# One set of seven PSUM banks, held as two three-bank tiles and one single tile, for every stage of an attention and gMLP block; output weights loaded in 14 pieces

## The chip, the core and the metric

The program runs on one core of a Trainium2 chip. The metric is the device time of one execution, in microseconds (us). The engines are TensorE (PE in the profile, with its weight loads as PEld), VectorE (DVE), ScalarE (ACT), GpSimd (POOL) and SyncE (SP, which here only issues transfers). Each engine works through its own list of instructions in order, and semaphores tie the lists together: an instruction that carries a wait holds up everything behind it on its engine.

## The reference

A sequence of 2048 tokens of width 448 goes through an attention block and then through a gMLP block, both with a layer norm whose shift and scale come from a small conditioning vector:

```
mod = silu(c) @ w_mod                        # sa, ca, ga, sb, cb, gb
h = layernorm(x) * (1 + ca) + sa
x = x + ga * attention(h)                    # 16 heads of 28, softmax over 2048 keys, then @ wo
h = layernorm(x) * (1 + cb) + sb
z = gelu(h @ w_in); z1, z2 = z[:, :896], layernorm(z[:, 896:])
g = w_sp @ z2 + b_sp                         # 2048 x 2048 mixing over the tokens
x = x + gb * ((z1 * g) @ w_out)
```

All of it is float32; most products are made of parts of float32r operands (a high part and a low part).

## The kernel before

The order of every engine's work is the order in which the Python code issues it; a recording layer adds the semaphores. It looks at which tile an instruction reads or writes, and makes a later user of that tile wait for an earlier one on another engine.

The stages, with the names that the profile shows:

- **Projection.** Values `pv`, queries and keys `pq` (`qk_unit`: groups of 11 matmuls into one PSUM bank, then read by ACT). From about 82 us on, the first score rows (`m_first`) stand between the matmuls of the remaining `qk_unit` groups.
- **Attention.** The loop runs over units `u`, 16 key tiles for each of 16 heads. A unit issues, in turn, four matmuls `st_ps` (`s_mm`; ACT reads each with an exponential into `P`) and four matmuls `mt` of a head 20 units later (`m_mm`; DVE reads each and keeps the row maximum in `pm`). Every second unit ends with the products of `P` and the values, `o_ps` (`pv_mm`). Two units, with 16 matmuls of `st_ps` and `mt` and one burst of `o_ps`, are called a pair below. The last 20 units have no `mt`.
- **Output projection, input projection, gate halves.** `wo_ps`, `z1_ps`, `z2_ps`: 11 matmuls into a bank, then a read by DVE or ACT.
- **Mixing.** The product with `w_sp` is built from 26 block products (`MIX`), each of four steps; step `g` runs from 0 to 103. `mix_step` issues nine matmuls into three banks of `accs`, and three more where the step also carries a piece of the last 128 columns (`F6_AT`). `w_load` brings raw blocks (`raw_sp`, five buffers), `w_split` makes high and low parts in `heapB`, and `evac` adds three banks at once to the result.
- **Output.** `y_part`: 21 matmuls for each of 16 token tiles into `y_ps`, then an add by DVE and a store.

All stages but the last two take their PSUM from `bank()`, which returns one of seven banks. In the first stages the list `banks` makes the seven go round; in attention the class `First` chooses the bank that a small table of due times says comes free first. Each call makes a new tile of one bank:

```
        return ring.tile([128, 512], F32, name=name, tag=f"b{k}")
```

So the tile that a matmul writes holds one bank, and what the matmul waits for is the reader of the tile that held this bank before, seven or so matmuls ago. Before the mixing the pool is closed, `accs` is made in a new one of eight banks (tiles of 3, 3, 1 and 1 banks), and after it that pool is closed too and `y_ps` gets a third one.

Of the kernel before, what the change touches and what calls it, by code (L numbers as in the profile page):

```python
# [8 lines left out]
F32 = mybir.dt.float32  # L9
F32R = mybir.dt.float32r  # L10
# [3 lines left out]
PSUM = bass.MemoryType.PSUM  # L14
DRAM = bass.MemoryType.DRAM

S, D, H, DH, FH = 2048, 448, 16, 28, 896
# [49 lines left out]
MIX = (  # L67
    (((T0, 4, 7, 1), (T1, 0, T0, 1)), T1, 1, 6, ((1, 1, -1), (1, 3, -1))),
    ((), T0, 1, 2, ((1, 0, 1),)),
    (((ONCE, 3, T1, 1),), ONCE, 1, 3, ((0, 2, 1),)),  # L70
    (((T1, 1, 2, 1), (ONCE, T1, T0, -1)), ONCE, 1, 11, ((0, 0, -1),)),
    (((ONCE, 0, T1, 1),), ONCE, -1, 19, ()),
    ((), T1, 1, 12, ((0, 1, 1), (1, 1, -1))),
    ((), 3, 1, 18, ((0, 0, -1), (0, 1, -1))),
    ((), 6, 1, (2, 1), ((1, 1, 1),)),
# [24 lines left out]
def tile_adaln_mha_gmlp(ctx, tc, x, wqkv, wo, w_in, w_spT, b_sp, w_out, cT, w_mod0, w_mod, out):  # L100
    nc = tc.nc
    ctx.enter_context(tc.manual_schedule())
    pe, dve, act, pool, sp = nc.tensor, nc.vector, nc.scalar, nc.gpsimd, nc.sync
# [11 lines left out]
    wo2_scr = scr.tile([2, 7, 128, D], F32, name="wo2_scr")  # L115
# [18 lines left out]
    def hview(heap, off, a, b):  # L134
        return heap[:, off : off + a * b].rearrange("p (a b) -> p a b", b=b)
# [68 lines left out]
    ps = ctx.enter_context(ExitStack())  # L204
    ring = ps.enter_context(tc.tile_pool(name="ring", bufs=1, space=PSUM))
    ps_o = ps.enter_context(tc.tile_pool(name="ps_o", bufs=1, space=PSUM))
# [17 lines left out]
    wms, xts, raws = {}, {}, {}  # L224


    banks, mode = list(range(7)), [None]

    def bank(name):
        k = mode[0](name) if mode[0] else banks[0]  # L230
        banks.remove(k)
        banks.append(k)
        return ring.tile([128, 512], F32, name=name, tag=f"b{k}")

    def load_mod(pair, eng):
        for k in range(4):
# [57 lines left out]
    accs = {}  # L294
# [552 lines left out]
    def w_block(k, j, kt):  # L847
        r = (4 * ROWS[k] + kt) * 128
        return w_spT[r : r + 128, j * 512 : (j + 1) * 512]
# [3 lines left out]
    def ws_tiles(i):  # L853
        if not ws_raw:
            ws_raw.append(dpool.tile([128, 7, 512], F32, name="ws_raw", tag="heapF"))
            ws_raw.append(spool.tile([128, 6, 512], F32, name="ws_raw2"))
        k = i % 6 if i < 100 else 3 + i % 3
        return [ws_raw[k // 3][:, 2 * (k % 3) + j, :] for j in range(2)]

    def ws_load(i):  # L860
# [113 lines left out]
    for u in range(NU + 1):  # L974
# [7 lines left out]
        if u % 2 and NU - LEAD < u < NU - 1:  # L982
            k = (u - NU + LEAD) // 2
# [26 lines left out]
    heapA = fh.tile([128, 8 * 896], F32R, name="heapA")  # L1010
# [161 lines left out]
    wouts = {}  # L1172
# [42 lines left out]

    wp = ctx.enter_context(tc.tile_pool(name="wp", bufs=4))
    FG = [slice(0, 384), slice(384, 768), slice(768, 896)]
    NM, KS = len(MIX), 4 * len(MIX)

    z6h = wp.tile([128, NT, 128], F32R, name="z6h", bufs=1)  # L1220
    heapA = fh.tile([128, 8 * 896], F32R, name="heapA2", tag="heapA")
    heapB2, tbuf = [], []
# [23 lines left out]
        return tbuf[1][:, f * D : (f + 1) * D]  # L1246

    def wouts_l(f):
        return tbuf[1][:, 3136 + f * D : 3136 + (f + 1) * D] if f < 4 else heapA[:, (f - 4) * 768 : (f - 4) * 768 + D]

    def wouts_load(i):
        if i == 0:
            tbuf.append(wp.tile([128, 5120], F32R, name="wouts", tag="tw", bufs=1))
            sp.dma_start(hview(tbuf[1], 0, 7, D).bitcast(F32), wo2_scr[0].rearrange("f p n -> p f n"))
            sp.dma_start(hview(tbuf[1], 3136, 4, D).bitcast(F32), wo2_scr[1, 0:4].rearrange("f p n -> p f n"))
        else:
            for f in range(4, 7):
                sp.dma_start(wouts_l(f).bitcast(F32), wo2_scr[1, f])

    zt = [dpool.tile([128, 8 * 896], F32, name=f"z2{i}", tag=f"heapD{i}") for i in range(2)]  # L1260
    z2 = [zt[i // 8][:, i % 8 * FH : (i % 8 + 1) * FH] for i in range(NT)]
# [1 line left out]
    once = []  # L1263
# [9 lines left out]
    def z_sum(p):  # L1273
        if p >= NM:
            return
        for d, a, b, op in MIX[p][0]:
            if d == ONCE:
                once[:] = [wp.tile([128, 4, 384], F32, name="once", bufs=1)]
            dve.tensor_tensor(out=z_reg(d), in0=z_reg(a), in1=z_reg(b), op=ALU.add if op > 0 else ALU.subtract)

    def z_parts(p):
# [20 lines left out]
        sub(dve, lo, src, hi)  # L1302

    F6_AT = {}
    for tb, gs, shared in (
        (1, range(4, 28, 2), 7),
        (2, (32, 34, 36, 38, 44, 45, 47, 48, 50, 51, 53, 54), 10),
        (0, [g for g in range(56, 80) if g % 3 != 1], None),
        (3, [g for g in range(80, 96) if g % 4 != 3], 24),
    ):  # L1310
        own = [k for k in (0, 3, 1, 2) if shared is None or k != MIX[shared][3][0]]
        for i, g in enumerate(gs):
            F6_AT[g] = (tb, own[i // 4], i % 4, False)
        if shared is not None:
            for kt in range(4):
                F6_AT[4 * shared + kt] = (tb, MIX[shared][3][0], kt, True)

    raws, wsp = {}, {}

    def w_load(g):  # L1320
        if g >= KS:
            return
        v, kt = MIX[g // 4][3], g % 4
        raws[g] = [wp.tile([128, 512], F32, name="raw_sp", bufs=5)]
        if isinstance(v, int):
            sp.dma_start(raws[g][0], ws_scr[4 * v + kt])
            if kt < 2:
                raws[g].append(w_part("p"))
                sp.dma_start(raws[g][1].bitcast(F32), wl_scr[2 * v + kt])
        else:  # L1330
            sp.dma_start(raws[g][0], w_block(*v, kt))
        if g in F6_AT and not F6_AT[g][3]:
            tb, k, kt, _ = F6_AT[g]
            raws["f", g] = [wp.tile([128, 512], F32, name="raw_sp", bufs=5)]
            sp.dma_start(raws["f", g][0], w_block(k, tb, kt))

    def w_split(g):
# [58 lines left out]
        if t in (13, 15):  # L1396
            w_split((t - 13) // 2)
    ph4.close()
    ps.close()
    pm = ctx.enter_context(ExitStack())  # L1400
    accs = pm.enter_context(tc.tile_pool(name="accs", bufs=1, space=PSUM))
    accs = [accs.tile([128, n, 512], F32, name=f"acc_{i}") for i, n in enumerate((3, 3, 1, 1))]

    cE = fh.tile([128, 4 * 896], F32, name="cE", tag="heapE")
    cC = fh.tile([128, 4 * 896], F32, name="cC", tag="heapC")
# [42 lines left out]
    z1s, nz = {}, [0, 0]  # L1448

    def z1_load():  # L1450
        if nz[0] < len(gates):
            f, tb = gates[nz[0]]
            z1s[f, tb] = wp.tile([128, 512], F32, name="z1l", tag="raw_sp", bufs=5)
            sp.dma_start(z1s[f, tb], z1_scr[f * 128 : (f + 1) * 128, tb * 512 : (tb + 1) * 512])
            nz[0] += 1

# [18 lines left out]
    ts_order = [8, 9, 10, 11, 4, 5, 6, 7, 12, 13, 14, 15, 0, 1, 2, 3]  # L1475
    x2t = {}

    def x2_load(t):
        x2t[t] = wp.tile([128, 512], F32, name="x2l", tag="raw_sp", bufs=5)[:, :D]
        sp.dma_start(x2t[t], x2_scr[t * 128 : (t + 1) * 128, :])  # L1480

    def y_part(t, end=False):
        ts, uT = slice(t % 4 * 128, t % 4 * 128 + 128), uTs[t // 4]
        y = ring.tile([128, 512], F32, name="y_ps", tag=f"y{ts_order.index(t) % 8}")
        for f in range(7):
            pe.matmul(y[:, :D], uT[:, f, ts], wouts_h(f), start=f == 0, stop=False)  # L1486
            pe.matmul(y[:, :D], uT[:, 7 + f, ts], wouts_h(f), start=False, stop=False)  # L1487
            pe.matmul(y[:, :D], uT[:, f, ts], wouts_l(f), start=False, stop=f == 6)  # L1488
        o = x2t.pop(t)
        for c, eng in ((slice(0, D), act),) if not end else ((slice(0, D // 2), act), (slice(D // 2, D), sp)):  # L1490
            dve.tensor_tensor(out=o[:, c], in0=o[:, c], in1=y[:, c], op=ALU.add)  # L1491
            eng.dma_start(out[t * 128 : (t + 1) * 128, c], o[:, c])

    GATE_AT = (71, 73, 75, 77, 79, 81, 82, 83, 94, 99, 100, 101, 102, 103)
    SPLIT_AT = {92: (6,), 96: (3, 4, 5), 98: (0, 1, 2)}

    for g in range(KS):
        p, kt = divmod(g, 4)
        w_load(g + 4)
        w_split(g + 2)  # L1500
        if kt == 0:
            if p:
                z_hi(p + 1)
                evac(p - 1)
        elif kt == 1 and p:
            z_lo(p + 1)
        elif kt == 2:
            z_sum(p + 2)
        if g == 5:
            z6_split(3)  # L1510
        if g < 4:
            b_load(utile(6, g), g)
        if g + 2 in GATE_AT:
            z1_load()
        if g in GATE_AT:
            gate()
        if g == 80:
            wouts_load(0)
        if g == 100:
            wouts_load(1)  # L1520
        if g in SPLIT_AT:
            u_split(2, SPLIT_AT[g])
        if g >= KS - 2:
            z1_load()
            x2_load(8 + g - (KS - 2))
        mix_step(g)

    evac(NM - 1)
    pm.close()
    ps2 = ctx.enter_context(ExitStack())  # L1530
    ring = ps2.enter_context(tc.tile_pool(name="ring2", bufs=1, space=PSUM))
    parts = {0: (1, (0, 1, 2)), 1: (1, (3, 4, 5)), 2: (1, (6,)), 4: (3, (3, 4, 5)), 5: (3, (0, 1, 2)), 6: (3, (6,))}
    parts.update({8: (0, (0, 1, 2)), 9: (0, (3, 4, 5)), 10: (0, (6,))})
    for k, t in enumerate(ts_order):
# [59 lines left out]
```

## Time and profile before

| | |
|---|---|
| median of three runs | 1409.01 us (1405.46 to 1410.49) |
| profiled execution, its own time | 1407.85 us |
| its span in the profile | 1405.9 us |
| PE busy | 1379.5 us, 98% |
| DVE busy | 1069.5 us, 76% |
| ACT busy | 805.4 us, 57% |
| POOL busy | 360.3 us, 26% |
| granted PE clock, mean of the span | 0.993 |

A busy PE means that some matmul was between its start and its modelled end; matmuls overlap in their pipeline, so the step from one start to the next is shorter than the duration of one. In the rows, `out<-in` names the tile written and the tiles read, and "waited for" names the work whose end released an engine.

### The profile page before, as it was taken

The page shows a single profiled execution, that of the slowest core. Times are in us where ns is not written, and L with a number is a line of the kernel's source. Part 1 is how long each engine was busy: PE and PEld are TensorE (multiplying, and loading weights), DVE is VectorE, ACT ScalarE, POOL GpSimd, SP SyncE. Part 2 cuts the span into 40 slices and gives each one's busy share as a digit, 9 for nine tenths or more (in the row PEclk, how much of TensorE's full clock was granted, in tenths as well). Part 3 has the DMA queues.
Part 4 walks back from the last instruction along what each step waited for, and adds up shares of the span by engine and source line. Part 5 has one row for each costly group of instructions (what it writes and reads, how often), then busy time and mean ns, then how long its engine had stood idle before and what let it go on. Part 6 is the DMA issues. An engine that isn't in the chain of part 4 may idle for free. (4 is left out here: it accounts for less than half of the span.)

```text
span 1405.9 us, 20520 instructions
## 1 busy us (share of the span) xinstructions
PE 1379.5 (98%) x7098; PEld 977.2 (70%) x7098; DVE 1069.5 (76%) x1688; ACT 805.4 (57%) x1472; POOL 360.3 (26%) x367
## 2 busy tenths in 40 slices
PE   9999999999999999999999999999999999978998
PEld 8888655555555555555555555888988888856798
DVE  7898888888888888888878842852478778976653
ACT  6633667777776667777766788553245545533311
POOL 2144344344444356546530021000110000000000
PEclk9999999999999999999999999999999999999999
DMA  8464766777676667777663012537307656767553
GB/s 293 140 176 167 212 183 204 208 216 230 201 238 199 205 206 243 219 228 228 202 188 84 22 31 74 184 127 234 112 16 246 203 178 204 235 207 238 173 155 125
DMA packets 136931, 254.28 MB, mean 181 GB/s; under 512 B 21688, under 2 KB 37178, under 8 KB 134282
## 3 DMA queue, kind: packets, MB, share of 16 engines
q1 hardware_dynamic: 134110, 248.79, 57.0%
q10 hardware_dynamic: 2718, 4.19, 0.8%
q8 instruction: 56, 0.92, 0.3%
q14 instruction: 47, 0.39, 0.1%
HBM read 174.53 MB, written 73.59 MB: 176 GB/s over the span
## 5 line engine op out<-in xcount | busy, mean ns | idle before, releaser
L713 DVE TENSOR_REDUCE pm<-mt 128x1 f32<-128x512 f32 x1024 | 631.4, 682 | 86.8 <-PE mt L708 86.7
L744 ACT ACTIVATE P<-st_ps 128x512 f32<-128x512 f32 x1024 | 515.7, 622 | 205.8 <-PE st_ps L740 204.9
L740 PE MATMUL st_ps<-qst,kst 128*128 128x512 f32 x1024 | 406.7, 407 | 0.0
L708 PE MATMUL mt<-kst,qst 128*128 128x512 f32 x1024 | 402.6, 393 | 0.0
L740 PEld LDWEIGHTS st_ps<-qst,kst 128*128 128x128 f32 x1024 | 191.8, 188 | 140.5 <-issue 93.1
L755 PE MATMUL o_ps<-P,V 128*32 128x512 f32 x2048 | 246.2, 598 | 0.0
L708 PEld LDWEIGHTS mt<-kst,qst 128*128 128x128 f32 x1024 | 193.0, 188 | 32.9
L868 POOL TENSOR_TENSOR ws_raw<-ws_raw 128x512 f32<-128x512 f32 x112 | 143.8, 1289 | 188.8 <-DMA ws_raw<-in_w_spT_dram 96.0
L1342 ACT ACTIVATE heapB<-raw_sp 128x512 fp32r<-128x512 f32 x156 | 96.6, 629 | 124.4 <-PE acc L1425 68.6
L755 PEld LDWEIGHTS o_ps<-P,V 128*32 128x32 f32 x2048 | 53.5, 109 | 121.9 <-issue 116.7
L1423 PE MATMUL acc<-heapB,heapA 128*128 128x512 f32 x312 | 123.7, 397 | 9.5 <-ACT heapB L1342 8.9
L1425 PE MATMUL acc<-heapB,heapA 128*128 128x512 f32 x312 | 123.4, 395 | 0.0
L150 DVE TENSOR_TENSOR heapB<-raw_sp,heapB 128x512 fp32r<-128x512 f32 x112 | 75.0, 688 | 47.1 <-ACT heapB L1342 46.4
L1424 PE MATMUL acc<-heapB,heapA 128*128 128x512 f32 x222 | 88.0, 396 | 6.7 <-DVE heapB L150 6.7
L1423 PEld LDWEIGHTS acc<-heapB,heapA 128*128 128x128 f32 x312 | 59.6, 191 | 24.4 <-ACT heapB L1342 10.9
L1425 PEld LDWEIGHTS acc<-heapB,heapA 128*128 128x128 f32 x312 | 59.7, 191 | 12.4
L403 PE MATMUL pq<-heapD,heapD 128*128 128x512 f32 x196 | 61.8, 390 | 0.0
L150 POOL TENSOR_TENSOR ws_raw<-ws_raw 128x512 fp32r<-128x512 f32 x44 | 56.6, 1287 | 3.5
L1424 PEld LDWEIGHTS acc<-heapB,heapA 128*128 128x128 f32 x222 | 42.3, 191 | 16.7 <-DVE heapB L150 7.9
L784 POOL TENSOR_TENSOR osb<-osb,rb 128x512 f32<-128x512 f32 x15 | 19.2, 1282 | 111.2 <-DMA rb<-r_scr 65.9
L170 POOL TENSOR_TENSOR rsz<-rsz,mhalf 128x1 f32<-128x1 f32 x16 | 14.2, 890 | 118.1 <-DVE rsz L169 118.1
L1361 ACT ACTIVATE z<-z_ps 128x448 f32<-128x448 f32 x32 | 17.4, 545 | 46.8 <-PE z_ps L1358 46.8
(220 smaller groups left out, 1653.8 us busy)
## 6 DMA issues: line engine op xcount, KB each, us to landing
ws_raw<-in_w_spT_dram SPq DMA_DIRECT2D x136, 256.0 KB
ws_scr<-ws_raw SPq DMA_DIRECT2D x112, 256.0 KB
ws_raw<-ws_scr SPq DMA_DIRECT2D x88, 256.0 KB
raw_sp<-ws_scr SPq DMA_DIRECT2D x88, 256.0 KB
raw_sp<-in_w_spT_dram SPq DMA_DIRECT2D x68, 256.0 KB
wl_scr<-ws_raw SPq DMA_DIRECT2D x44, 256.0 KB
kst<-qk_scr SPq DMA_DIRECT2D x45, 224.0 KB
qst<-qk_scr SPq DMA_DIRECT2D x45, 224.0 KB
```

Source lines behind the costliest of these rows:

```text
L150: eng.tensor_tensor(out=dst, in0=a, in1=hi.bitcast(F32), op=ALU.subtract)
L403: pe.matmul(pq, wqk[:, b, m * 128 : (m + 1) * 128], hT[g][:, a, :], start=j == 0, stop=j == NST - 1)
L708: pe.matmul(mt, qst[h % 3][:, t * 128 : (t + 1) * 128], kst[h % 3][:, kb * 512 : (kb + 1) * 512], start=True, stop=True)
L713: dve.tensor_reduce(out=pms[h][:, t, kb : kb + 1], in_=mt, axis=AX.X, op=ALU.max)
L740: pe.matmul(st, kst[h % 3][:, kt * 128 : (kt + 1) * 128], qst[h % 3][:, qb * 512 : (qb + 1) * 512], start=True, stop=True)
L744: act.activation(p, st, AF.Exp, scale=SCALE)
L755: pe.matmul(otile[h][32 * qb : 32 * qb + 32, :], V[:, kt, h, :], ptiles.pop((u, qb)), start=kt == 0, stop=kt == NT - 1)
L868: pool.tensor_tensor(out=a, in0=a, in1=b, op=ALU.add if W_SUMS[v][2] > 0 else ALU.subtract)
L1342: act.activation(hi, raw[0], AF.Copy)
L1423: pe.matmul(o, zh[:, c], hi, start=p < 2 and kt == 0, stop=False, skip_group_check=p > 1)
L1424: pe.matmul(o, zh[:, c], lo, start=False, stop=False, skip_group_check=p > 1)
L1425: pe.matmul(o, zl[:, c], hi, start=False, stop=kt == 3, skip_group_check=p > 1)
```

## The change

Five things are changed.

1. `bank()` no longer makes tiles. Three tiles are made once: `ring_a` and `ring_b` of three banks each, `ring_c` of one. `bank()` returns a view of one bank of these. Which bank is chosen is decided by the same lists and tables.
2. The pool stays open to the end. The mixing sums `accs` are the tiles `ring_a`, `ring_b`, `ring_c` and the bank that the values' products used; `y_part` takes views of the same banks.
3. The output weights are loaded by 14 transfers of one 128x448 piece each, at steps 46 to 99 of the mixing, in place of two large and three small ones at steps 80 and 100.
4. The buffers of the raw mixing blocks are seven, not five; the pieces of the last 128 columns are placed by a rule that keeps them apart; the gates (`GATE_AT`) stand at other steps.
5. The operand buffers of the weight sums (`ws_tiles`) go round by six to the end. Before, they went round by three from the hundredth on, and a block was loaded over one that had not yet been stored.

```
+    sums_a, sums_b = (ring.tile([128, 3, 512], F32, name=f"ring_{n}") for n in "ab")
+    ring_c = ring.tile([128, 512], F32, name="ring_c")
+    ring_v = [sums_a[:, k, :] for k in range(3)] + [sums_b[:, k, :] for k in range(3)] + [ring_c]
...
-        return ring.tile([128, 512], F32, name=name, tag=f"b{k}")
+        return ring_v[k]
...
-        k = i % 6 if i < 100 else 3 + i % 3
+        k = i % 6
...
+    WOUT_AT = [(46, 0, 0), (49, 0, 1), (52, 0, 2), (55, 0, 3), (58, 0, 4), (61, 0, 5), (64, 0, 6)]
...
+    def wouts_load(g):
+        for at_g, i, f in WOUT_AT:
+            if at_g == g:
...
+                sp.dma_start((wouts_l if i else wouts_h)(f).bitcast(F32), wo2_scr[i, f])
...
+        if f6_items and g not in F6_AT and (f6_items[0][0] in (1, 2) or g >= 47):
+            near = [range(max(a, 0), a + 3) for a in (g - 2, g - 1, g)]
+            if all(sum(own6(i) for i in w) < 2 and sum(lows(i) for i in w) < 4 for w in near):
+                F6_AT[g] = f6_items.pop(0)
...
-        raws[g] = [wp.tile([128, 512], F32, name="raw_sp", bufs=5)]
+        raws[g] = [wp.tile([128, 512], F32, name="raw_sp", bufs=RAWS)]
...
-    ps.close()
-    pm = ctx.enter_context(ExitStack())
-    accs = pm.enter_context(tc.tile_pool(name="accs", bufs=1, space=PSUM))
-    accs = [accs.tile([128, n, 512], F32, name=f"acc_{i}") for i, n in enumerate((3, 3, 1, 1))]
+    accs = [sums_a, sums_b, ring_c[:, None, :], ps_o.tile([128, 512], F32, name="acc6", tag="o")[:, None, :]]
...
-        y = ring.tile([128, 512], F32, name="y_ps", tag=f"y{ts_order.index(t) % 8}")
+        y = y_banks[ts_order.index(t) % 8]
...
-    pm.close()
-    ps2 = ctx.enter_context(ExitStack())
-    ring = ps2.enter_context(tc.tile_pool(name="ring2", bufs=1, space=PSUM))
+    y_banks = [accs[i][:, n, :] for i, n in ((0, 0), (0, 1), (0, 2), (2, 0), (3, 0), (1, 0), (1, 1), (1, 2))]
```

What moves in the built program can be read on PE in a pair of the attention. Before, the eight matmuls of its first unit stand as below; `st_ps` is read by ACT, `mt` by DVE, and "waits" names the engine whose semaphore the matmul waits for.

```order
L740 MATMUL st_ps<-qst_875,kst_874 128x512 [waits Activation_49]
L708 MATMUL mt<-kst_870,qst_871 128x512 [waits DVE_49]
L740 MATMUL st_ps<-qst_875,kst_874 128x512 [waits Activation_49]
L708 MATMUL mt<-kst_870,qst_871 128x512 [waits DVE_49]
L740 MATMUL st_ps<-qst_875,kst_874 128x512 [waits Activation_49]
L708 MATMUL mt<-kst_870,qst_871 128x512 [waits DVE_49]
L740 MATMUL st_ps<-qst_875,kst_874 128x512 [waits DVE_49]
L708 MATMUL mt<-kst_870,qst_871 128x512 [waits Activation_49]
```

By the semaphore values, each of these waits is for a reader of a matmul issued six or more places earlier. The same place after the change, on PE, with L743 for `st_ps` and L711 for `mt` (the pair's first twelve matmuls):

```order
L743 MATMUL ring_a<-qst_839,kst_838 128x512 [waits DVE_49]
L711 MATMUL ring_c<-kst_834,qst_835 128x512
L743 MATMUL ring_a<-qst_839,kst_838 128x512 [waits Activation_49]
L711 MATMUL ring_b<-kst_834,qst_835 128x512 [waits DVE_49]
L743 MATMUL ring_b<-qst_839,kst_838 128x512 [waits DVE_49]
L711 MATMUL ring_a<-kst_834,qst_835 128x512 [waits Activation_49]
L743 MATMUL ring_b<-qst_839,kst_838 128x512 [waits Activation_49]
L711 MATMUL ring_a<-kst_834,qst_835 128x512 [waits DVE_49]
L743 MATMUL ring_c<-qst_839,kst_838 128x512
L711 MATMUL ring_a<-kst_834,qst_835 128x512 [waits DVE_49]
L743 MATMUL ring_b<-qst_839,kst_838 128x512 [waits Activation_49]
L711 MATMUL ring_b<-kst_834,qst_835 128x512 [waits Activation_49]
```

The matmuls stand in the same order and go to the same choice of banks. What moved is the wait: it is for the reader of the last matmul that wrote the same *tile*, whichever of its three banks that was. The third row waits for the reader of the first, the fifth for that of the fourth, the seventh for that of the fifth.

The other engine whose list moves is SP. In the second half of the mixing, before, the output weights stand as two large transfers between the loads of the blocks:

```order
L1454 DMA z1l<-z_scr 128x512
L1254 DMA wouts<-wo_scr 128x7x448
L1255 DMA wouts<-wo_scr 128x4x448
L1326 DMA raw_sp<-ws_scr 128x512
L1329 DMA heapA_11258<-wl_scr 128x512
```

After the change the first two of the fourteen pieces, some 30 steps earlier, stand on SP like this:

```order
L1264 DMA wouts<-wo_scr 128x448
L1343 DMA raw_sp<-ws_scr 128x512
L1352 DMA raw_sp<-in_w_spT_dram 128x512
L1343 DMA raw_sp<-ws_scr 128x512
L1346 DMA heapA_9074<-wl_scr 128x512
L1343 DMA raw_sp<-ws_scr 128x512
L1346 DMA heapB_9376<-wl_scr 128x512
L1352 DMA raw_sp<-in_w_spT_dram 128x512
L1264 DMA wouts<-wo_scr 128x448
```

Between two pieces there are now six or more loads of blocks.

More of the change, by code (lines that the diff above doesn't have):

```diff
@@ L1217, in tile_adaln_mha_gmlp @@
     FG = [slice(0, 384), slice(384, 768), slice(768, 896)]
-    NM, KS = len(MIX), 4 * len(MIX)
+    NM, KS, RAWS = len(MIX), 4 * len(MIX), 7
     z6h = wp.tile([128, NT, 128], F32R, name="z6h", bufs=1)
@@ L1248, in wouts_l @@
     def wouts_l(f):
[L1249 to L1258, printed above, removed]
+        return tbuf[1][:, 3136 + f * D : 3136 + (f + 1) * D] if f < 4 else tbuf[2][:, (f - 4) * D : (f - 3) * D]
+    WOUT_AT = [(46, 0, 0), (49, 0, 1), (52, 0, 2), (55, 0, 3), (58, 0, 4), (61, 0, 5), (64, 0, 6)]
+    WOUT_AT += [(68, 1, 0), (72, 1, 1), (76, 1, 2), (80, 1, 3), (95, 1, 4), (97, 1, 5), (99, 1, 6)]
+    def wouts_load(g):
+        for at_g, i, f in WOUT_AT:
+            if at_g == g:
+                if (i, f) == (0, 0):
+                    tbuf.append(wp.tile([128, 5120], F32R, name="wouts", tag="tw", bufs=1))
+                if (i, f) == (1, 4):
+                    tbuf.append(wp.tile([128, 1536], F32R, name="wouts2", tag="once", bufs=1))
+                sp.dma_start((wouts_l if i else wouts_h)(f).bitcast(F32), wo2_scr[i, f])
     zt = [dpool.tile([128, 8 * 896], F32, name=f"z2{i}", tag=f"heapD{i}") for i in range(2)]
@@ L1277, in z_sum @@
             if d == ONCE:
-                once[:] = [wp.tile([128, 4, 384], F32, name="once", bufs=1)]
+                once[:] = [wp.tile([128, 1536], F32, name="once", tag="once", bufs=1).rearrange("p (t c) -> p t c", c=384)]
             dve.tensor_tensor(out=z_reg(d), in0=z_reg(a), in1=z_reg(b), op=ALU.add if op > 0 else ALU.subtract)
@@ L1304, in tile_adaln_mha_gmlp, with lows, own6 @@
     F6_AT = {}
[L1305 to L1316, printed above, removed]
+    for tb, shared in ((1, 7), (2, 10), (3, 24)):
+        for kt in range(4):
+            F6_AT[4 * shared + kt] = (tb, MIX[shared][3][0], kt, True)
+    def lows(g):
+        return int(isinstance(MIX[g // 4][3], tuple) or g % 4 > 1) + own6(g)
+    def own6(g):
+        return int(g in F6_AT and not F6_AT[g][3])
+    f6_items = [
+        (tb, k, kt, False)
+        for tb, shared in ((1, 7), (2, 10), (0, None), (3, 24))
+        for k in (0, 3, 1, 2)
+        if shared is None or k != MIX[shared][3][0]
+        for kt in range(4)
+    ]
+    for g in range(4, KS - 4):
+        if f6_items and g not in F6_AT and (f6_items[0][0] in (1, 2) or g >= 47):
+            near = [range(max(a, 0), a + 3) for a in (g - 2, g - 1, g)]
+            if all(sum(own6(i) for i in w) < 2 and sum(lows(i) for i in w) < 4 for w in near):
+                F6_AT[g] = f6_items.pop(0)
+    assert not f6_items
     raws, wsp = {}, {}
@@ L1333, in w_load @@
             tb, k, kt, _ = F6_AT[g]
-            raws["f", g] = [wp.tile([128, 512], F32, name="raw_sp", bufs=5)]
+            raws["f", g] = [wp.tile([128, 512], F32, name="raw_sp", bufs=RAWS)]
             sp.dma_start(raws["f", g][0], w_block(k, tb, kt))
@@ L1452, in z1_load @@
             f, tb = gates[nz[0]]
-            z1s[f, tb] = wp.tile([128, 512], F32, name="z1l", tag="raw_sp", bufs=5)
+            z1s[f, tb] = wp.tile([128, 512], F32, name="z1l", tag="raw_sp", bufs=RAWS)
             sp.dma_start(z1s[f, tb], z1_scr[f * 128 : (f + 1) * 128, tb * 512 : (tb + 1) * 512])
@@ L1478, in x2_load @@
     def x2_load(t):
-        x2t[t] = wp.tile([128, 512], F32, name="x2l", tag="raw_sp", bufs=5)[:, :D]
+        x2t[t] = wp.tile([128, 512], F32, name="x2l", tag="raw_sp", bufs=RAWS)[:, :D]
         sp.dma_start(x2t[t], x2_scr[t * 128 : (t + 1) * 128, :])
@@ L1492, in y_part @@
             eng.dma_start(out[t * 128 : (t + 1) * 128, c], o[:, c])
-    GATE_AT = (71, 73, 75, 77, 79, 81, 82, 83, 94, 99, 100, 101, 102, 103)
+    GATE_AT = (67, 70, 71, 74, 75, 79, 82, 83, 87, 91, 94, 95, 99, 101)
     SPLIT_AT = {92: (6,), 96: (3, 4, 5), 98: (0, 1, 2)}
@@ L1516, in tile_adaln_mha_gmlp @@
             gate()
[L1517 to L1520, printed above, removed]
+        wouts_load(g)
         if g in SPLIT_AT:
```

## The prediction

> **What bounds the kernel now.** I read the page first: PE is busy for nearly the whole span, and no other engine comes near it.
>
> ```profile
> span 1405.9 us, 20520 instructions
> PE 1379.5 (98%) x7098; PEld 977.2 (70%) x7098; DVE 1069.5 (76%) x1688; ACT 805.4 (57%) x1472; POOL 360.3 (26%) x367
> ```
>
> Then the busy time by stretches, cut where the stages change: the first score rows among the projections, the attention with both kinds of score matmul, its last 20 units, and the mixing. Columns are length, PE busy, granted clock, DMA share and GB/s.
>
> ```profile
> 82.00:145.00 63.00, 63.00 (x280) 1.00 0.54 174
> 145.00:826.00 681.00, 678.35 (x3780) 1.00 0.64 192
> 826.00:867.00 41.00, 41.00 (x252) 1.00 0.08 19
> 1056.00:1333.00 277.00, 260.31 (x1116) 0.98 0.67 213
> ```
>
> Attention is half of the time, and PE has no gap in it but one. There are (256 - 20) / 2 = 118 pairs of units in 681.00 us, 5.77 us each. The waits of PE in that stretch, and in the mixing and output:
>
> ```profile
> PE mtp L729 <- POOL mxp L150: 2.7, 1, 2.7
> ...
> PE acc L1423 <- ACT heapB L1342: 8.9, 4, 5.2
> PE acc L1424 <- DVE heapB L150: 6.7, 3, 3.6
> PE y_ps L1486 <- DVE cE L1413: 1.8, 1, 1.8
> ```
>
> PE runs at its own rate in attention because the matmul that it starts never needs a bank whose reader is not long done. The timeline of one pair shows that rate (start, duration):
>
> ```profile
> 399.84 0.50 PE L740 MATMUL st_ps<-qst,kst 128*128 128x512 f32 x1
> 400.18 0.40 PE L708 MATMUL mt<-kst,qst 128*128 128x512 f32 x1
> 400.42 0.40 PE L740 MATMUL st_ps<-qst,kst 128*128 128x512 f32 x1
> 400.65 0.40 PE L708 MATMUL mt<-kst,qst 128*128 128x512 f32 x1
> ...
> 403.73 1.92 PE L755 MATMUL o_ps<-P,V 128*32 128x512 f32 x16
> 405.58 0.50 PE L740 MATMUL st_ps<-qst,kst 128*128 128x512 f32 x1
> ```
>
> A step is 0.23 us, the burst of `o_ps` 1.85; after a restart the first matmul takes 0.50, and the next follows 0.34 later. The rate holds only while steps need not wait for readers.
>
> **The shared tiles: the price of one wait.** The change makes matmuls wait for the reader of the last matmul in the same three-bank tile. A reader's duration (min/median/max, ns), the hand-over from matmul to reader, and that from DVE to PE:
>
> ```profile
> L713 DVE TENSOR_REDUCE pm<-mt x1024: 627/681/693, 83.4 to 825.9; 128x1 f32<-128x512 f32 x171
> ...
> L744 ACT ACTIVATE P<-st_ps x1024: 589/617/728, 145.9 to 867.3; 128x512 f32<-128x512 f32 x171
> ...
> 141.28 0.39 PE L708 MATMUL mt<-kst,qst 128*128 128x512 f32 x1
> ...
> 141.71 1.37 DVE L713 TENSOR_REDUCE pm<-mt 128x1 f32<-128x512 f32 x2 [0.21 <-PE mt L708]
> ...
> 1331.89 1.75 DVE L1413 TENSOR_TENSOR cE<-cE,acc 128x1536 f32<-128x1536 f32 x1 [2.19 <-PE acc L1425]
> ...
> 1333.70 0.47 PE L1486 MATMUL y_ps<-wouts,uT 128*128 128x448 f32 x1 [1.85 <-DVE cE L1413]
> ```
>
> The reader starts 0.04 us after the matmul's end (141.67 to 141.71), and PE starts 0.06 after the reader's (1333.64 to 1333.70). From a restarted matmul to the next one in its tile it is thus 0.50 + 0.04 + 0.68 + 0.06 = 1.28 us through DVE, and 1.22 through ACT. Where such a matmul stood directly behind, it started 0.23 later before; so the wait adds 1.05 or 0.99.
>
> **How many.** I counted, in the built order of the 118 pairs, how many places before the waiting matmul the one stands whose reader it waits for: 473 directly ahead, 408 two places, 263 three, 98 four. Nothing can hide the 473: at 1.02 each they add 482 us, the lower bound. Counting each of the others as if nothing between had waited (0.79, 0.56 and 0.33) adds 322, 147 and 32, so 984 us is the upper bound. Per pair that is 5.77 + 4.1 = 9.9 to 5.77 + 8.3 = 14.1 us.
>
> For the value between I take the pair shown with the change and follow it by hand, from its first start at 0, each matmul at the later of its predecessor plus 0.23 (0.34 after a restart) and of the reader it waits for: 0, 0.23, 1.22, 1.56, 2.84, 3.18, 4.06, 4.46, then 4.80, 5.74, 6.08, 7.30, 8.58, 8.92, 9.15 and 10.20 for the last four of the first twelve and the four behind them (the thirteenth waits for DVE's reader of the twelfth, the sixteenth for that of the fourteenth). The burst starts at 10.54 and the next pair 1.85 later: 12.4 us for 5.77. That is near the middle of the bounds (12.0), and I take it: +6.63 a pair, 118 pairs, **+782 us**. DVE and ACT, at 4 x 2 x 0.68 = 5.4 us or less a pair, have slack, and do not bound it.
>
> **The clock.** PE would then stand still for 4.7 us in the 12.4, and the granted clock can answer that. Short stretches around PE's stalls before the change, each followed by its successor:
>
> ```profile
> 732.10:735.50 3.40, 0.94 (x12) 1.00 0.97 357
> 735.50:738.90 3.40, 3.20 (x9) 0.51 0.15 54
> ...
> 1251.00:1254.30 3.30, 1.55 (x8) 1.00 0.01 2
> 1254.30:1257.70 3.40, 3.40 (x8) 0.52 0.75 208
> 1257.70:1261.10 3.40, 2.16 (x10) 0.98 0.47 148
> 1261.20:1264.60 3.40, 2.13 (x9) 1.00 0.89 259
> ```
>
> A stretch of 3.4 us with PE busy 28% or 47% is followed by one at half clock; with 63% and 64% it isn't; a busy stretch at half clock gives the full clock back. In the pair above PE is busy 62% overall but only (10.54 - 4.74) / 10.54 = 55% outside the burst, between the two. By matmuls the answer is clearer: the throttled 1251 stretch had 8, the spared ones 10 and 9, and outside the burst the pair has 16 x 3.4 / 10.5 = 5.2. So I expect the clock to fall. At half clock the rows are
>
> ```profile
> 735.74 0.77 PE L740 MATMUL st_ps<-qst,kst 128*128 128x512 f32 x1
> 736.32 0.63 PE L708 MATMUL mt<-kst,qst 128*128 128x512 f32 x1
> 736.74 0.63 PE L740 MATMUL st_ps<-qst,kst 128*128 128x512 f32 x1
> ```
>
> so the link grows by 0.27 to 1.55 (DVE) or 1.49 (ACT), the step to 0.43 (0.58 after a restart), the burst to an estimated 3.7, twice the row. The same pair, followed again, has its burst at 13.6 and takes 17.3 us, with PE busy 69% outside the burst, enough to get the clock back. It would go to and fro, at half the time each: 2 / (1/12.4 + 1/17.3) = 14.4 us a pair, clock about 0.75. That makes 118 x 8.68 = **+1024 us** instead of 782.
>
> The Trainium skill (TensorE: Matmul & The Clock Gate, Why this matters for your kernels) puts the danger at idle gaps above about 3 us between bursts; by that rule no wait here is long enough and the pairs stay at 12.4 us, the first rival below. The 1251 stretch does not agree: its idle time is 1.75 us in all. The same page (A second HAM failure mode) tells of a kernel whose clock oscillated from short stalls as PSUM banks went round.
>
> **The other stages** take the same waits. In the ramp 26 directly behind and some 20 two or three back: 40 us between bounds of 27 and 43. Before it 16 directly behind: 20. In the last 20 units 33: 35. In `wo_ps`, `z1`, `z2` and `y_ps` together 34, with readers of 0.55 us and more: 35. For instance the reads of `z2`:
>
> ```profile
> L1361 ACT ACTIVATE z<-z_ps 128x448 f32<-128x448 f32 x32 | 17.4, 545 | 46.8 <-PE z_ps L1358 46.8
> ```
>
> Together +130 us at full clock (100 to 145), and 0.27 more on half of about 120 waits, +146, with the clock going to and fro.
>
> **The mixing and the output.** The sums were three-bank tiles before, so no wait is added there. The spread loads, seven raw buffers and the moved pieces can remove at most PE's waits above, 8.9 + 6.7 + 1.8 = 17 us, and some 5 of lost clock behind them (0.02 of 277); SP has the same bytes to issue and nine transfers more, each as short as the others, and the gates at new steps may bring a wait of DVE back. I take -12, between -22 and +5. The corrected operand buffers wait no more than before and lie under attention: 0; if PE were idle there, their loads have still more time.
>
> **Sum**, on the profiled execution's own 1407.85 (the median is 1.2 higher, too little to matter): 1407.85 + 1024 + 146 - 12 = 2566 us.
>
> **Rivals.** *The clock holds.* If the gate answers to something the short gaps don't trip (62% of the pair is busy, near the 63% that was spared), the sum is 1407.85 + 782 + 130 - 12 = 2308. *The clock stays down.* If getting it back needs more than the 69% of a half-clock pair (the row that regained it had 94%), pairs cost up to 17.3: 1407.85 + 118 x 11.5 + 162 - 12 = 2915; against it, each burst of `o_ps` fills most of a stretch. *The waits are hidden and the change is faster.* The score matmuls could be waiting for readers that are already done, as before; then only the mixing's 12 to 22 us remain and the time is 1386 to 1396. This decides if the link were below two steps, 0.46 us; the reader alone takes 0.62. *The change doesn't do what it says*, one pool without the waits: the order shows them; the time would be 1396 too. *Waits partly hidden*: only those directly behind count, 1407.85 + 482 + 100 - 12 = 1978.
>
> **Chances.** The forecast 0.57; the clock holds 0.27; the clock stays down, over 2780, 0.11; partly hidden 0.03; hidden or not as said 0.02. From the first case I keep 2400 to 2780 (pairs of 13 to 16.2 us), from the second 2250 to 2400; the range 2250 to 2780 leaves out the third and the small ones and some of the edges. A run of this kernel can tell about 0.3% (4 us) from no change. Faster 0.02, the same 0.01, slower 0.97.
>
> **What would show it.** In the changed profile PE waits in attention for DVE's `pm` and ACT's `P` some 8 times a pair, for 0.5 to 1 us; the busy shares of DVE and ACT fall by nearly half; the score stage takes about 1700 us with a clock of about 0.75 (0.95 or more: the second case; under 0.65: the third). If starts of matmuls in attention are still 0.23 apart, the whole argument is wrong.

## The result, and the profile after

The changed kernel takes 2697.35 us (median; 2687.67 to 2710.52) beside 1407.33 for the kernel before (1405.46 to 1410.49) on the same chip: 1.917 times as long (95% interval 1.911 to 1.922). Its profiled execution took 2694.57 us. The page's first rows and its row of the granted clock:

```profile
span 2692.8 us, 20562 instructions
...
PE 2082.4 (77%) x7098; PEld 1072.9 (40%) x7098; DVE 1144.3 (42%) x1688; ACT 896.1 (33%) x1472; POOL 356.1 (13%) x367
...
PEclk8888765768777666666796776665776799999999
```

PE has the same 7098 matmuls and is busy with them for 2082 us instead of 1380. Two things lengthen that: the clock is lower (0.770 in the mean of the span, 0.993 before), and a matmul that starts after a wait no longer overlaps the one before it (`turns`, below, shows this alone). Beside that PE now stands idle for 610 us. The shares of DVE and ACT have fallen from 76% to 42% and from 57% to 33%. To see where, the stretches of before, cut at the ends of stages (up to the first exponential; the pairs; the last 20 units; output and input projection with gate halves; mixing; output). Columns are length, PE busy, clock, DMA share, GB/s:

```profile
0.00:145.40 145.40, 143.49 (x703) 1.00 0.59 193
145.40:825.90 680.50, 677.85 (x3777) 1.00 0.64 192
825.90:867.30 41.40, 41.40 (x254) 1.00 0.08 19
867.30:1052.80 185.50, 184.90 (x905) 1.00 0.41 138
1052.80:1331.00 278.20, 262.63 (x1125) 0.98 0.66 211
1331.00:1405.90 74.90, 69.22 (x340) 0.99 0.44 138
```

And the changed kernel, cut at the same events:

```profile
0.00:248.00 248.00, 184.66 (x703) 0.90 0.35 116
248.00:2006.60 1758.60, 1287.56 (x3774) 0.69 0.25 74
2006.60:2113.40 106.80, 78.08 (x250) 0.67 0.03 8
2113.40:2352.60 239.20, 204.08 (x908) 0.94 0.32 108
2352.60:2608.00 255.40, 255.40 (x1127) 1.00 0.71 233
2608.00:2692.80 84.80, 72.67 (x340) 0.98 0.34 111
```

Stage by stage: +102.6, **+1078.1**, +65.4, +53.7, **-22.8**, +9.9, together +1286.9. The pairs carry five sixths of it; a pair takes 1758.6 / 118 = 14.90 us instead of 5.77. The mixing is shorter, and PE is busy in all of it. The waits of PE (us in total, times, longest) name what holds the pairs up; these rows are of the whole span:

```profile
PE ring_b L743 <- DVE pm L716: 105.9, 139, 0.9
PE ring_b L711 <- ACT P L747: 102.3, 155, 0.8
PE ring_a L743 <- DVE pm L716: 85.3, 112, 0.9
PE ring_a L711 <- ACT P L747: 74.8, 118, 0.8
PE ring_b L743 <- ACT P L747: 40.2, 87, 1.0
PE ring_a L743 <- ACT P L747: 39.1, 89, 0.9
PE ring_a L711 <- DVE pm L716: 36.4, 95, 0.6
...
PE ring_b L711 <- DVE pm L716: 11.0, 29, 0.6
```

Of these 824 waits, 780 lie in the pairs: 6.6 a pair, 466 us together, 0.60 us each, none over 0.9. That is nearly all of the 471 us that PE stands idle there (1758.60 - 1287.56). A score matmul waits for DVE's or ACT's reader of another bank, because both banks lie in `ring_a` or in `ring_b`; `ring_c`, one bank alone, is in no row. A burst of `o_ps` and part of the pair behind it in the timeline (start, duration, idle time before):

```profile
1001.83 3.64 PE L758 MATMUL o_ps<-P,V 128*32 128x512 f32 x16
...
1005.93 0.39 PE L711 MATMUL ring_b<-kst,qst 128*128 128x512 f32 x1
1007.10 0.50 PE L743 MATMUL ring_b<-qst,kst 128*128 128x512 f32 x1 [0.78 <-DVE pm L716]
1008.29 0.50 PE L711 MATMUL ring_b<-kst,qst 128*128 128x512 f32 x1 [0.69 <-ACT P L747]
...
1010.17 0.79 PE L743 MATMUL ring_a<-qst,kst 128*128 128x512 f32 x1 [0.92 <-DVE pm L716]
1011.65 0.79 PE L711 MATMUL ring_a<-kst,qst 128*128 128x512 f32 x1 [0.69 <-ACT P L747]
...
1013.62 0.79 PE L711 MATMUL ring_b<-kst,qst 128*128 128x512 f32 x1 [0.75 <-ACT P L747]
1015.20 0.79 PE L743 MATMUL ring_b<-qst,kst 128*128 128x512 f32 x1 [0.79 <-DVE pm L716]
```

From one matmul to the next in its tile it is 1.19 us through ACT at full clock (1007.10 to 1008.29), and at half clock, where a matmul that waited takes 0.79 and not 0.50, 1.48 through ACT and 1.58 through DVE. The burst ahead of the pair, at half clock, takes 3.64.

### The profile page after: what moved, and what is told of

Same layout as the page of the kernel before. It is cut to its first block, busy times and chain, and to the rows that moved or that the text cites. A ratio compares the mean times of both kernels' runs of the same rounds, so it can differ in the third digit from the quotient of the medians.

```text
span 2692.8 us, 20562 instructions
## 1 busy us (share of the span) xinstructions
PE 2082.4 (77%) x7098; PEld 1072.9 (40%) x7098; DVE 1144.3 (42%) x1688; ACT 896.1 (33%) x1472; POOL 356.1 (13%) x367
## 5 line engine op out<-in xcount | busy, mean ns | idle before, releaser
L716 DVE TENSOR_REDUCE pm<-ring_a 128x1 f32<-128x512 f32 x459 | 317.1, 691 | 490.7 <-PE ring_a L711 490.5
L747 ACT ACTIVATE P<-ring_b 128x512 f32<-128x512 f32 x512 | 305.5, 597 | 626.3 <-PE ring_b L743 626.3
L716 DVE TENSOR_REDUCE pm<-ring_b 128x1 f32<-128x512 f32 x390 | 269.5, 691 | 460.5 <-PE ring_b L711 460.1
L747 ACT ACTIVATE P<-ring_a 128x512 f32<-128x512 f32 x414 | 247.1, 597 | 522.9 <-PE ring_a L743 522.6
L743 PE MATMUL ring_b<-qst,kst 128*128 128x512 f32 x512 | 301.1, 588 | 148.5 <-DVE pm L716 105.9
L758 PE MATMUL o_ps<-P,V 128*32 128x512 f32 x2048 | 405.6, 935 | 0.0
L711 PE MATMUL ring_a<-kst,qst 128*128 128x512 f32 x459 | 267.7, 583 | 112.7 <-ACT P L747 74.8
L743 PE MATMUL ring_a<-qst,kst 128*128 128x512 f32 x414 | 248.7, 601 | 125.0 <-DVE pm L716 85.3
L711 PE MATMUL ring_b<-kst,qst 128*128 128x512 f32 x390 | 222.5, 570 | 115.0 <-ACT P L747 102.3
L743 PEld LDWEIGHTS ring_b<-qst,kst 128*128 128x128 f32 x512 | 124.1, 242 | 338.8 <-DVE pm L716 173.0
L743 PEld LDWEIGHTS ring_a<-qst,kst 128*128 128x128 f32 x414 | 99.4, 240 | 312.9 <-DVE pm L716 150.8
L711 PEld LDWEIGHTS ring_a<-kst,qst 128*128 128x128 f32 x459 | 111.9, 244 | 242.6 <-ACT P L747 143.9
L711 PEld LDWEIGHTS ring_b<-kst,qst 128*128 128x128 f32 x390 | 92.8, 238 | 222.2 <-ACT P L747 182.3
L711 PE MATMUL ring_c<-kst,qst 128*128 128x512 f32 x175 | 91.5, 523 | 0.0
```

The lines of the kernel that those rows point to most:

```text
L711: pe.matmul(mt, qst[h % 3][:, t * 128 : (t + 1) * 128], kst[h % 3][:, kb * 512 : (kb + 1) * 512], start=True, stop=True)
L716: dve.tensor_reduce(out=pms[h][:, t, kb : kb + 1], in_=mt, axis=AX.X, op=ALU.max)
L743: pe.matmul(st, kst[h % 3][:, kt * 128 : (kt + 1) * 128], qst[h % 3][:, qb * 512 : (qb + 1) * 512], start=True, stop=True)
L747: act.activation(p, st, AF.Exp, scale=SCALE)
L758: pe.matmul(otile[h][32 * qb : 32 * qb + 32, :], V[:, kt, h, :], ptiles.pop((u, qb)), start=kt == 0, stop=kt == NT - 1)
```

## The experiments

**Each bank in a tile of its own.** The first question is whether the shared tiles are the whole loss. In `own_tiles` the changed kernel gets the PSUM arrangement of before back, and keeps the rest:

```diff
...
-        return ring_v[k]
+        return ring.tile([128, 512], F32, name=name, tag=f"b{k}")
...
+    ps.close()
...
-    accs = [sums_a, sums_b, ring_c[:, None, :], ps_o.tile([128, 512], F32, name="acc6", tag="o")[:, None, :]]
+    accs = [accs.tile([128, n, 512], F32, name=f"acc_{i}") for i, n in enumerate((3, 3, 1, 1))]
...
-        y = y_banks[ts_order.index(t) % 8]
+        y = ring.tile([128, 512], F32, name="y_ps", tag=f"y{ts_order.index(t) % 8}")
```

> The changed kernel with its PSUM arrangement taken back: each call of the bank function makes a tile of one bank again, the mixing sums and the outputs get pools of their own as before; the 14 pieces, the seven raw buffers, the moved pieces and gates and the corrected operand buffers stay. Theory (the added waits come from the three-bank tiles alone): the attention is back at 680 us with a granted clock of 1.0, the mixing stays at about 256 us in place of 278, so 1407 - 22 = 1385 us (1380 to 1395). Rival (the mixing gained because PSUM was not changed over between stages): the mixing returns to 278 and the time is 1405 to 1410. Rival (some of the loss comes from the operand buffers or the moved loads): over 1420.

1383.81 us, 0.983 of before (0.982 to 0.985). Its pairs, its mixing and its output:

```profile
146.80:823.70 676.90, 676.90 (x3777) 1.00 0.64 193
1050.60:1305.80 255.20, 255.19 (x1126) 1.00 0.71 233
1305.80:1382.00 76.20, 70.70 (x340) 0.97 0.37 123
```

PE is busy in all of the first two. `shared_only` is the opposite: the kernel before with only the shared tiles and the one pool.

```diff
...
-        return ring.tile([128, 512], F32, name=name, tag=f"b{k}")
+        return ring_v[k]
...
-    accs = [accs.tile([128, n, 512], F32, name=f"acc_{i}") for i, n in enumerate((3, 3, 1, 1))]
+    accs = [sums_a, sums_b, ring_c[:, None, :], ps_o.tile([128, 512], F32, name="acc6", tag="o")[:, None, :]]
```

> The kernel before with nothing but the shared tiles and the one PSUM pool. Theory (they cost all of the loss, and the rest of the change gave 22 us back in the mixing): 2697 + 22 = 2719 us (2700 to 2745), attention at 14.9 us a pair with a clock of about 0.69, mixing near 278 us. Rival (the moved loads carry a part of the loss): below 2650.

2722.67 us, 1.934 of before (1.930 to 1.937). Its pairs and its mixing:

```profile
250.50:2012.30 1761.80, 1291.28 (x3774) 0.69 0.25 74
2358.10:2635.30 277.20, 263.22 (x1128) 0.98 0.68 212
```

So the loss belongs to the shared tiles with their one pool (+1315 us without any other edit; `two_bank` and `seven_bank` below wait in the same way with the pools of before, so the tiles are enough), and the gain of the mixing to the other edits (277.20 with the old mixing, 255.20 with the new one).

**How far ahead the awaited matmul stands.** If the price comes from waiting for the last matmul of one's tile, it must follow the width of the tile and the order of tiles. `turns` keeps the shared tiles of the change, but takes the banks so that `ring_a`, `ring_b`, `ring_c` come in turn: no matmul of the pairs waits for the one directly ahead or two places ahead, 1464 for the one three places ahead.

```diff
+    class Turn:
...
+            while True:
+                self.i += 1
+                free = [k for k in banks if k // 3 == self.i % 3 and k not in held]
+                if free:
+                    return free[0]
...
-    first_free = mode[0] = First()
+    first_free = mode[0] = Turn()
```

> The changed kernel, tiles as changed, but in attention the banks are chosen so that the three tiles take turns: a, b, c, a, b, c. Counted in its order, 1464 score matmuls wait for the reader three places ahead and none for one or two places ahead. Theory (distance sets the price): three matmuls per link of 1.25 us, 0.42 each, so 16 x 0.42 + 1.85 + 0.3 = 8.8 us a pair in place of 14.9, 118 x 6.1 = 720 us less: about 1975 us (1850 to 2100), and with PE busy some three quarters the clock is above 0.9. Rival (the number of waits counts, about as many as in the changed kernel): 2600 or more. Rival (the clock gate answers to any waits): clock still near 0.7, over 2200.

1867.33 us, 1.327 of before (1.325 to 1.328). The pairs, and the two largest waits:

```profile
250.60:1246.30 995.70, 903.55 (x3775) 1.00 0.44 131
```

```profile
PE ring_c L743 <- DVE pm L716: 20.1, 87, 0.3
PE ring_c L711 <- ACT P L747: 15.0, 61, 0.3
```

8.44 us a pair at full clock, with waits of 0.3 us or less: the same tiles and the same matmuls, in another rotation, make a kernel that is 830 us faster. The two rows are of `ring_c`, which is one bank: this rotation uses it for every third matmul, so these waits are for the reader of the same bank. And the pairs of `turns` show what a wait costs beside idle time. They take 318.8 us more than those of `own_tiles`, at clock 1.00 in both; only 92.2 of that is idle time, and 226.7 is busy time for the same matmuls, many of which no longer overlap. In `two_bank` and `seven_bank` the width is changed, with the rest as in `own_tiles`: three tiles of two banks and one of one, or all seven in one tile.

```diff
+    twos = [ring.tile([128, 2, 512], F32, name=f"two_{i}") for i in range(3)]
+    ring_v = [t[:, k, :] for t in twos for k in range(2)] + [ring.tile([128, 512], F32, name="one")]
```

```diff
+    seven = ring.tile([128, 7, 512], F32, name="seven")
+    ring_v = [seven[:, k, :] for k in range(7)]
```

> As own_tiles, but the seven banks of the stages before the mixing are held as three tiles of two banks and one of one; the pools are opened and closed as before the change. Counted in its order, in the attention pairs 223 score matmuls wait for the reader directly ahead, 225 two, 252 three, 176 four and 120 five places ahead. Theory (distances in a tile set the price): between 223 x 1.02 = 227 and 616 us more at full clock, middle 420, some 60 in the other stages, 1384 + 480 = 1864, and with PE idle some 40% of the pair outside the bursts a part of the time at half clock, about 150 more: 2010 us (1850 to 2200). Rival (the one pool kept open, not the tiles' width, brings the waits): 1384.

> As two_bank, but all seven banks are one tile. Counted: 1756 of the 1888 score matmuls in pairs wait for the reader directly ahead. Theory: at full clock 16 x 1.25 + 2.2 = 22 us a pair, PE busy under 45%, so half clock but for some stretches at the bursts, with 16 x 1.52 + 3.7 = 28: some 27 us a pair, 118 x 21 = 2480 more than own_tiles, and about 400 in the other stages: 4260 us (3800 to 4600). Rival (what costs is the choice of banks in three tiles, not the waiting): near 2700.

One run each: 2017.75 and 4327.54 us. The pairs of the first, and of the second:

```profile
200.20:1395.40 1195.20, 911.18 (x3775) 0.92 0.36 109
```

```profile
393.20:3561.90 3168.70, 1866.01 (x3774) 0.53 0.14 41
```

With one, two, three and seven banks in a tile a pair takes 5.74, 10.13, 14.90 and 26.85 us, close to what was expected for each, though two of these are single runs.

**The clock.** The theory says that the idle time of PE lowers its clock, so matmuls that do nothing useful should make the kernel faster if they fill that time. `filled` is the changed kernel with a product of zeros, added into `o_ps`, ahead of most score matmuls (1712 in all):

```diff
...
+    def filler(moving):
+        for t in otile.values():
+            pe.matmul(t, zeros, moving, start=False, stop=False)
...
+        filler(kst[h % 3][:, kb * 512 : (kb + 1) * 512])
...
+        filler(qst[h % 3][:, qb * 512 : (qb + 1) * 512])
```

> The changed kernel with one more matmul ahead of every score matmul: a zero matrix times the key or query tile, added to the values' product bank, where it adds nothing (left out where no such bank is open, 2 units in 16). Some 1700 matmuls that nobody needs. Theory (PE's idle share lowers the clock): they fill the waits, PE is busy 80% outside the bursts, the clock stays above 0.93; the pair followed by hand with them takes 13.6 us at full clock in place of the 14.9 measured, so the kernel gets faster by 100 to 200 us, 2530 us (2450 to 2620). Rival (the clock does not answer to the idle share, or the added work counts in full): 1700 x 0.23 = 390 us and more on top, over 2900.

> The same additional matmuls in own_tiles, where no score matmul waits. Both theories: PE is the bound there, so each costs its step, 1700 x 0.23 = 390 us: about 1775 us, clock 1.0. It prices the addition made in filled.

2522.05 us, 1.792 of before (1.789 to 1.795): with 1712 matmuls more it is 175 us faster than the changed kernel. The same matmuls in `own_tiles` (`filled_own`, one run) give 1782.13 us, 398 slower than without. The pairs of `filled`, and of `filled_own`:

```profile
247.80:1856.20 1608.40, 1329.84 (x5415) 0.95 0.27 81
```

```profile
145.50:1206.50 1061.00, 1061.00 (x5415) 1.00 0.41 123
```

In `filled` the clock is 0.95 and not 0.69, and a pair takes 13.63 us. What remains above 5.77 is waiting, lost overlap and the fillers' own work; what they removed is most of the loss of clock.

**The mixing.** Which of the edits removed the 23 us? `own_two_loads` is `own_tiles` with the output weights loaded as before; `own_five` has five raw buffers again.

```diff
...
-        wouts_load(g)
+        if g == 80:
+            wouts_load(0)
+        if g == 100:
+            wouts_load(1)
```

> As own_tiles, but the output weights are loaded as before the change, by two large transfers at step 80 and three at step 100. Theory (what the mixing gained is the wait for raw blocks behind the large transfers, about 11 us of it after step 80): 1385 + 11 = 1396 us (1390 to 1402). Rival (the seven buffers and moved pieces hide the large transfers too): within 3 us of own_tiles.

```diff
-    NM, KS, RAWS = len(MIX), 4 * len(MIX), 7
+    NM, KS, RAWS = len(MIX), 4 * len(MIX), 5
```

> As own_tiles, but with five raw buffers in place of seven. Theory (the spread loads and pieces carry the gain, buffers are spare): within 4 us of own_tiles, about 1387. Rival (the two buffers carry it): 1395 to 1407.

1387.66 us (0.986 of before, 0.985 to 0.988) and 1386.54 us (0.985, 0.984 to 0.987). The mixing of the first, and of the second:

```profile
1051.10:1309.40 258.30, 256.06 (x1125) 1.00 0.71 230
```

```profile
1049.40:1307.80 258.40, 256.07 (x1125) 1.00 0.73 229
```

Each alone gives back about 3 us of the 23. The forecast that the old loads would give back 11 us (1390 to 1402 in all) missed. Either the moved pieces of the last 128 columns and the gates carry the rest, or each of the two edits covers for the other; the two were not undone together, so this stays open.

`own_tiles`, the change without its shared tiles, is the fastest kernel measured here.

## Why the prediction was right, and where it was off

**The mechanism** was the one given: matmuls wait for the reader of another bank in the same tile. The predicted 8 waits a pair of 0.5 to 1 us are 6.6 of 0.60 on average, and the two opposite experiments show that no other edit makes them. The rivals in which the waits are hidden, partly hidden or not there are ruled out, and so is the one in which the clock holds: the pairs had 0.69 (about 0.75 was expected), above the 0.65 under which the clock would have stayed down.

**The link** was priced at 1.22 us through ACT and, at half clock, 1.49 and 1.55; the timeline shows 1.19, 1.48 and 1.58. Through DVE at full clock it was 1.28; the nine such steps of the pairs that start from a matmul that waited take 1.28 to 1.29. The burst at half clock was estimated at 3.7 and takes 3.64. The two prices of a pair worked out by hand, 12.4 us at full clock and 17.3 at half, also agree, taken together, with the measured total: a mean clock of 0.69 means half clock for 62% of the time, and 0.38 x 1758.6 / 12.4 + 0.62 x 1758.6 / 17.3 = 53.9 + 63.0 = 117 pairs, where there are 118.

**The clock's way back** is a step that was off. The prediction held that a stretch at half clock with PE busy 69% is "enough to get the clock back", and so gave each clock half of the time. Here is the changed kernel in consecutive stretches of 3.41 us, laid on the grid on which its clock changed, so that nearly every stretch shows one clock:

```profile
985.32:988.73 3.41, 2.37 (x8) 0.50 0.74 212
988.73:992.14 3.41, 3.41 (x17) 0.50 0.62 234
992.14:995.56 3.42, 2.81 (x11) 0.99 0.28 65
995.56:998.97 3.41, 1.98 (x5) 1.00 0.93 311
998.97:1002.38 3.41, 2.92 (x8) 0.51 0.67 230
...
1016.04:1019.45 3.41, 2.31 (x5) 0.50 0.00 0
1019.45:1022.86 3.41, 3.41 (x17) 0.50 0.02 5
1022.86:1026.28 3.42, 2.41 (x10) 0.99 0.00 0
```

Stretches at half clock that were busy 2.37 and 2.31 us of 3.41 (69% and 68%) are followed by half clock again. Only the full ones, where the burst of `o_ps` lies, are followed by full clock. At full clock 2.81 us (82%) keeps it and 1.98 (58%) loses it. I counted the 513 such stretches of the pairs: of 208 at half clock and less than 85% busy none got the clock back, of 110 above that 94 did; of 84 at full clock and less than 60% busy 81 lost it, of 111 above that 12 did. The way down was placed well (55% between a 47% that fell and a 63% that did not), the way up was set too low, though the stretches of before that got the clock back were busy 94% and 100% (the rows at 735.50 and 1254.30). The count sorts the stretches by busy share; whether the clock goes by that share or by something that goes with it was not separated. So half clock lasts 62% of the time and not 50%, and a pair takes 14.90 us and not 14.4: 54 of the 129 us by which the profiled time exceeds the forecast.

The Trainium skill (TensorE: Matmul & The Clock Gate, Why this matters for your kernels) asks, so that throughput does not drop in mid-kernel, that no idle gap between bursts exceed about 3 us. By this trace that is not enough: no wait in the pairs is over 0.9 us, and the clock is 0.69. The same page (What's actually happening) says that full rate comes after a busy window of about 3.4 us, sustained; by the counts above the trace agrees: below 85% busy no stretch brought the full clock back.

**The other stages** were put at +146 us and cost 231.6. Two things were sized too small. Before the first exponential (60 predicted, 102.6 measured) and in the projections some waits are not one link long, since the reader is itself late behind other work of its engine:

```profile
PE ring_b L406 <- DVE ql L150: 7.5, 3, 4.7
PE ring_b L833 <- DVE x L1036: 7.4, 2, 6.4
PE ring_b L388 <- ACT hfull L186: 4.9, 1, 4.9
```

The prediction had given each about 1 us. Before the wait of 4.7 us, for instance, DVE first fills `kst` and `qst` (two times 1.76 us, from 107.92 on) and only then reads the bank. And in the last 20 units (35 predicted, 65.4 measured) the clock was down to 0.67, lower than the half and half that was assumed. There, too, the prediction charged half clock only 0.27 us on every second wait and nothing for the steps and bursts between the waits. PE's busy time in these 20 units grew by 36.7 us (41.40 to 78.08); in all the other stages together its growth is 100.5 of the 231.6.

**The mixing and the output** were put at -12, between -22 and +5. The mixing alone gained 22.8, just beyond the far end of the range: the edits removed all of the 15.6 us in which PE was not busy there (278.20 - 262.63) and also 7.2 us of busy time (262.63 to 255.40), about what 13.7 us at half clock cost there (half of that, 6.8). The output is 9.9 us longer, which stood under the other stages; without the shared tiles it is 1.3 longer (76.20 in `own_tiles`).

The sum: 2566 + 54 (pairs) + 86 (other stages) - 11 (mixing) = 2695, the profiled execution. The largest miss is thus in the other stages, at 146 for 231.6, and the next is the clock of the pairs.

## What to carry to other kernels

In a layer like this one a wait goes by the tile that the program names, not by the bank in it: PSUM banks that are filled and read on their own belong in tiles of their own, and where they must share one, let the tiles take turns so that the awaited reader is old. Before and after such a change look at which semaphore values the matmuls wait for, since the order of the instructions and the choice of banks can stay as they were while the kernel becomes twice as slow. A short wait that repeats is paid three times: as idle time, as overlap that the matmuls behind it lose, and, where PE is idle enough, as a lower clock for all the work around it.

## What the runs showed of the hardware that was not expected

The clock has different marks on its way down and up: in stretches of 3.41 us it mostly falls below about 60% busy and comes back only at 85% or more, so a kernel between the two mostly keeps the clock that it last had. `seven_bank`, counted the same way, agrees: of 825 stretches at half clock below 85% none got the clock back, of 53 above 48 did, and all 48 at full clock were below 60% and lost it. The mark on the way down is not sharp: in `two_bank` 20 of 30 stretches between 55% and 60% kept the clock. And work without use can buy time: 1712 products of zeros lifted the clock of the pairs from 0.69 to 0.95 and made the kernel 175 us faster, while the same products cost 398 us where PE had no idle time.
